# Loading the last job's feed-forward weights in units of 1024 columns

## The chip, the cores and the metric

The kernel runs on one core of one Trainium2 chip. The metric is device time in microseconds of one execution; each kernel is run several times and the median counts. The core has a matrix engine (TensorE, PE; its weight loads are listed apart as PEld), a vector engine (VectorE, DVE), a scalar engine (ScalarE, ACT), GpSimd (POOL) and a queue engine (SyncE, SP) that issues most of the DMA transfers. All transfers run on 16 DMA engines that the queues share.

## What is computed

Two layers, each an attention with a recurrent memory followed by a gated feed-forward block, with the same weights in both layers:

```python
def _A_ref(x, mem0, Wq, Wk, Wv, Wo, seg_len):      # S = 2048, D = 576, H = 32, Dh = 128, M = 8, seg = 32
    mem = mem0
    for s in range(n_seg):                          # 64 segments, one after another
        h = concat([mem, x[segment s]])             # 40 rows
        q, k, v = h @ Wq, h @ Wk, h @ Wv
        p = softmax(where(mask, q @ k.T * scale, -1e9))
        o = (p @ v) @ Wo
        mem = o[:, :M]                              # handed to the next segment
        outs.append(o[:, M:])
def _B_ref(x, w1, w3, w2):                          # F = 4608
    return (silu(x @ w1) * (x @ w3)) @ w2

x = x + _A_ref(_layernorm(x), ...); x = x + _B_ref(_layernorm(x), ...)
x = x + _A_ref(_layernorm(x), ...); x = x + _B_ref(_layernorm(x), ...)
```

All inputs are bfloat16; `w1` and `w3` are 576 x 4608 and `w2` is 4608 x 576.

## The kernel before

The attention is a chain over 64 segments, so the kernel runs it in steps: step t works on segment t of the first layer and, eight steps later, on segment t - 8 of the second. There are 72 steps, 0 to 71; the last eight have the second layer alone. `step` builds the nodes of one step: QK (queries and keys of 32 heads in four groups of 8 heads; each group's main matmuls read chunks 0 to 7 of the tile W, QKt its chunk 8), SC (scores), softmax on DVE and ACT, TR (transpose), PV, WO (the output projection, one node for each group, WO0 to WO3) and VM/VX (values, from the tile WV).

The feed-forward block works on 128 rows at a time, in jobs (`job`). F is cut into 18 pairs of 128-column blocks (`pr`, 0 to 17); a node FF makes gate and up for one pair (16 matmuls over four 128-row chunks, 32 when its columns are split), FFt adds the last 64 of the 576 rows (4 matmuls), ACT and DVE make the product in HTT, and W2b multiplies two pairs (one `pp`) by `w2`. For most jobs the weights of one pair are brought by `load_w13` (two transfers of 256 KB, two of 32 KB into the tile W13) and `load_w2` (288 KB into W2C), in two buffers each.

The last job cannot start before the last step's attention is done. By then Wq and Wk in the tile W and Wv in the tile WV are no longer read, and the kernel loads most of the last job's weights over them. `tail_load(i, what, gate)` does it in eight units i of 512 columns (two pairs): `what` 0 brings W1 and W3 into the columns `i * 512` on of W, chunks 0 to 3 and 4 to 7, with the 64-row remainders in the two halves of chunk 8; `what` 1 brings W2 into WV. Unit 0 serves pairs 0 and 1, unit 7 pairs 14 and 15. Pairs 16 and 17 stay in W13 and W2C from the job before. The job before also uses unit 0, for its own last two pairs.

What holds a tail transfer: the reads of the old contents (QK of the group of heads in those columns; a group has 1024 columns of W, two units), the lane of its completion semaphore (SP's transfers take eight in turn, so a ninth waits for the landing of the first), and for `what` 0 a gate. The gate is a manual dependence of the unit's first transfer on a matmul node of the last step: unit 0 has none, unit 1 waits for WO1, units 2 to 7 for WO3. The order on TensorE is written out by hand, as letters in `FIRST`, `FOUR` and `LAST`; the orders of the other engines and of SP come from `plan`, which places each node at its earliest time by the given costs and priorities. Line 659 is the helper of every matmul, 662 of ACT, 665 of DVE, 668 of the transfers on SP.

Of the kernel before, what the change touches and what calls it, by code (L numbers as in the profile page):

```python
# [13 lines left out]
P = 128  # L14
R64 = 64
D = 576
# [231 lines left out]
def make_nodes(em, nseg, pools, o=Opt, dma_bw=230e3, load_bw=345e3):  # L248
# [4 lines left out]
    def node(*a, **k):  # L253
        n = Node(*a, **k)
        n.prio += 1e-9 * len(nodes)
        nodes.append(n)
        return n
# [5 lines left out]
    kb = lambda rows, cols: rows * cols * 2  # L263
# [9 lines left out]
    def load(name, nbytes, prio, fn, deps=()):  # L273
        return node("DMA", nbytes / load_bw, fn, deps=deps, prio=prio, name=name, lat=2.0)
# [208 lines left out]
    tail = []  # L483
# [3 lines left out]
    def job(j):  # L487
# [6 lines left out]
        s0 = 4 * j + 4 if j < ngrp else 4 * j - 4 + LAG  # L494
# [74 lines left out]
        if last:  # L569
            v_done, qk_done = last_reads  # L570
            me = steps[nst - 1]
            gates = {1: me["WO1"], **{i: me[f"WO{NG - 1}"] for i in range(2, 8)}}
            for i in range(8):
                g = gates.get(i)
                tail.append([load("tail", kb(128, c), s0 + o.tail_at + 0.01 * i, em.tail_load(i, what, g), deps=dep + [g])
                             for what, c, dep in ((0, 9 * 512, qk_done[i]), (1, 4 * 576, v_done))])
            shared.pop()()
        norm()
        if last:
# [29 lines left out]
    for t in range(nst):  # L609
        if t % 4 == 2 and (t + 2) // 4 < ngrp:  # L610
            x_in((t + 2) // 4)
        if t == LAG:
            ht_mem[t].append(node("DVE", 0.1, em.init_mem(1, LAG), deps=[m0e] + reads_ht.get(LAG - R_HT, []), prio=LAG - 2, name="m0"))
        if role(t) == 0 or t == 0:
            vx_pair(t - role(t), t - 1 + o.vx)
        step(t)
        if t % 4 == 1 and t // 4 < ngrp:
            x_res(t // 4)
        if t % 4 == 3:
            job((t + 1) // 4 - 1)  # L620
        elif t == nst - 1:
            job(nst // 4)
# [12 lines left out]
class Emitter:  # L635
# [139 lines left out]
    def tail_load(self, i, what, gate):  # L775

        def f(n):
            T = self.T
            fa = i * 512
            t13, t2 = T.W[:, :, fa:fa + 512], T.WV[:, i * 4 * D:(i + 1) * 4 * D].rearrange("p (b d) -> p b d", b=4)  # L780
            held = gate and what == 0

            def dma(*x):
                nonlocal held
                self.dma(*x)
                if held:
                    held = False
                    self.tc.add_manual_dep(self.last["SP"].ins, gate.inst.ins.name, self.pace_dep, reason="pace of the loads")

            if what == 0:  # L790
                for kind, wd in ((0, self.a.w1), (1, self.a.w3)):
                    dma(t13[:, 4 * kind:4 * kind + 4], wd[0:4 * P, fa:fa + 512].rearrange("(c p) f -> p c f", p=P))
                for kind, wd in ((0, self.a.w1), (1, self.a.w3)):
                    dma(t13[kind * R64:(kind + 1) * R64, 8], wd[4 * P:D, fa:fa + 512])
            else:
                dma(t2, self.a.w2[fa:fa + 512, :].rearrange("(b p) d -> p b d", p=P))
            for h in range(2):
                self.tail_w[2 * i + h] = (t13[:, :, h * 2 * P:(h + 1) * 2 * P], t2[:, 2 * h:2 * h + 2])
        return f
# [637 lines left out]
```

## Time and profile before

| what | us |
|---|---|
| median of 3 runs (lowest, highest) | 2650.18 (2648.84, 2653.23) |
| profiled execution | 2657.81 |
| its span, first to last instruction | 2656.0 |
| TensorE busy in the span | 2578.3 |
| VectorE busy | 2004.1 |
| ScalarE busy | 1242.3 |

The mean granted clock of TensorE was 0.992 of full speed. Times in the views below are microseconds from the start of the span. In the chain of waits each row has its start, its length and what the end of the kernel waited for then; "issue" is time in which the engine waited for nothing that the profile shows. In the timeline a row gives start, length, engine, line, operation, tiles and number of instructions, and in brackets the idle time before it with what ended it. In the DMA rows q1 is the queue of data transfers from SP and ACT, q8 that of instruction blocks; numbers are packets, MB and the share of the 16 engines. In the rows of stretches the busy time of each engine follows the length, then the granted clock, the DMA share and GB/s.

### The profile page before, as it was taken

The page shows a single profiled execution, that of the slowest core. Times are in us where ns is not written, and L with a number is a line of the kernel's source. Part 1 is how long each engine was busy: PE and PEld are TensorE (multiplying, and loading weights), DVE is VectorE, ACT ScalarE, POOL GpSimd, SP SyncE. Part 2 cuts the span into 40 slices and gives each one's busy share as a digit, 9 for nine tenths or more (in the row PEclk, how much of TensorE's full clock was granted, in tenths as well). Part 3 has the DMA queues.
Part 4 walks back from the last instruction along what each step waited for, and adds up shares of the span by engine and source line. Part 5 has one row for each costly group of instructions (what it writes and reads, how often), then busy time and mean ns, then how long its engine had stood idle before and what let it go on. Part 6 is the DMA issues. An engine that isn't in the chain of part 4 may idle for free.

```text
span 2656.0 us, 133410 instructions
## 1 busy us (share of the span) xinstructions
PE 2578.3 (97%) x59426; PEld 2216.6 (83%) x59426; DVE 2004.1 (75%) x5137; ACT 1242.3 (47%) x3495; POOL 335.2 (13%) x399
## 2 busy tenths in 40 slices
PE   6899999999999999999999999999999999999998
PEld 4788878888888888888888888888888888888887
DVE  4677777877787778778777877877787787777866
ACT  2555453444545444454544544454444445454443
POOL 1111111110101111010101101110110111011110
PEclk8899999999999999999999999999999999999999
DMA  9055746556554655555465555645565554554458
GB/s 322 4 153 150 182 101 152 128 131 157 117 141 108 152 135 126 155 128 139 109 143 134 138 146 125 146 106 151 122 147 139 132 140 106 129 139 131 130 155 244
DMA packets 690433, 371.48 MB, mean 140 GB/s; under 512 B 234328, under 2 KB 682592, under 8 KB 689216
## 3 DMA queue, kind: packets, MB, share of 16 engines
q1 hardware_dynamic: 686320, 355.08, 53.5%
q8 instruction: 464, 7.60, 1.2%
q0 software_dynamic: 3024, 6.93, 0.9%
q10 hardware_dynamic: 512, 0.94, 0.2%
q14 instruction: 113, 0.93, 0.1%
HBM read 306.72 MB, written 2.36 MB: 116 GB/s over the span
## 4 chain that ended last, share of the span: by engine, by line
PE 83%; DMA 9%; DVE 5%; ACT 1%; issue 1%; SPq 1%; POOL 0%; ACTq 0%; DVEq 0%; POOLq 0%
PE bank L659 83%; DMA PTS<-PB 5%; DMA W<-in_B_w_dram 1%; DMA W2C<-in_B_w_dram 1%; DVE STAT L665 1%; DMA WV<-in_A_Wv_dram 1%; DVE SME L665 1%; DVE PB L665 1%; SPq L668 1%; DVE V L665 0%; DMA W<-in_A_Wq_dram 0%; ACT V L662 0%; DVE XR L665 0%; DVE HTT L665 0%; DVE LNS L665 0%
## 5 line engine op out<-in xcount | busy, mean ns | idle before, releaser
L659 PEld LDWEIGHTS <-W 128*128 128x128 bf16 (+2 forms) x32464 | 1259.9, 100 | 118.1 <-issue 63.6
L659 PE MATMUL bank<-HT,W 128*128 128x80 bf16 (+3 forms) x23040 | 785.1, 197 | 16.1 <-issue 9.3
L659 PE MATMUL bank<-XTB,W 128*64 128x256 bf16 (+5 forms) x9424 | 658.9, 263 | 2.0 <-DMA W<-in_B_w_dram 2.0
L1093 POOL MEMSET PB<- 128x1024 bf16 x288 | 273.9, 951 | 1944.4 <-DMA PTS<-PB 1142.8
L662 ACT ACTIVATE QKT<-bank 128x256 bf16<-128x256 f32 (+4 forms) x1423 | 342.4, 320 | 246.4 <-PE bank L659 216.9
L659 PE MATMUL bank<-OT,WO 128*128 128x80 bf16 (+3 forms) x11520 | 421.2, 199 | 1.0 <-ACT OT L662 0.5
L662 ACT ACTIVATE V<-bank 64x512 bf16<-64x512 f32 (+1 forms) x605 | 339.6, 585 | 164.9 <-PE bank L659 158.4
L659 PEld LDWEIGHTS <-WO 128*128 128x128 bf16 (+1 forms) x11520 | 387.8, 102 | 34.0 <-issue 18.7
L659 PE MATMUL bank<-WV,HT 128*32 128x512 bf16 (+4 forms) x3768 | 370.4, 386 | 5.1 <-DMA WV<-in_A_Wv_dram 4.5
L659 PE MATMUL bank<-W2C,HTT 128*64 128x288 bf16 (+1 forms) x3216 | 321.8, 287 | 3.4 <-DMA W2C<-in_B_w_dram 2.8
L662 ACT ACTIVATE OT<-bank 128x320 bf16<-128x320 f32 x374 | 153.8, 437 | 313.2 <-PE bank L659 309.3
L665 DVE TENSOR_REDUCE STAT<-SME 104x8 f32<-104x320 f32 (+1 forms) x576 | 275.1, 478 | 27.9 <-ACT SME L662 22.3
L665 DVE TENSOR_TENSOR PB<-SME,STAT 40x128 bf16<-40x128 f32 (+4 forms) x912 | 275.4, 336 | 12.1 <-DVE STAT L665 0.4
L665 DVE SCALAR_TENSOR_TENSOR HTT<-HTT,bank 128x512 bf16<-128x512 bf16 (+1 forms) x324 | 201.5, 622 | 106.7 <-ACT HTT L662 103.7
L659 PEld LDWEIGHTS <-HT 128*32 128x32 bf16 (+4 forms) x3768 | 155.4, 100 | 145.2 <-issue 39.1
L659 PEld LDWEIGHTS <-HTT 128*64 128x64 bf16 (+1 forms) x3288 | 230.1, 105 | 40.8 <-issue 7.3
L662 ACT ACTIVATE HTT<-bank 128x512 bf16<-128x512 f32 (+1 forms) x324 | 173.9, 548 | 179.9 <-PE bank L659 178.3
L665 DVE SCALAR_TENSOR_TENSOR XR<-bank,XR 128x288 f32<-128x288 f32 x574 | 241.5, 447 | 14.4 <-PE bank L659 11.0
L662 ACT ACTIVATE SME<-SME 104x320 f32<-104x320 f32 (+1 forms) x288 | 135.1, 469 | 241.4 <-DVE SME L665 238.1
L665 DVE TENSOR_TENSOR HTT<-HTT,bank 128x512 bf16<-128x512 bf16 (+1 forms) x324 | 203.7, 629 | 33.0 <-PE bank L659 0.5
L665 DVE CAST QKT<-bank 128x192 bf16<-128x192 f32 (+2 forms) x497 | 141.4, 328 | 104.7 <-PE bank L659 102.5
L665 DVE CAST V<-bank 64x512 bf16<-64x512 f32 (+1 forms) x259 | 177.3, 684 | 36.9 <-PE bank L659 33.0
(60 smaller groups left out, 1394.4 us busy)
## 6 DMA issues: line engine op xcount, KB each, us to landing
W<-in_B_w_dram SPq DMA_DIRECT2D x608, 256.0 KB, 3.9
W2C<-in_B_w_dram SPq DMA_DIRECT2D x304, 288.0 KB, 3.5
W<-in_B_w_dram SPq DMA_DIRECT2D x608, 32.0 KB, 3.9
W<-in_B_w_dram SPq DMA_DIRECT2D x16, 512.0 KB, 8.3
WO<-in_A_Wo_dram SPq DMA_DIRECT2D x4, 1152.0 KB, 10.0
XR<-in_A_x_dram POOLq DMA_DIRECT2D x16, 288.0 KB, 4.0
WV<-in_B_w_dram SPq DMA_DIRECT2D x8, 576.0 KB, 7.3
W<-in_A_Wq_dram SPq DMA_DIRECT2D x16, 256.0 KB, 5.8
```

The source lines that it names most:

```text
L659: self.ch("PE", self.nc.tensor.matmul(out, lhsT=lhsT, rhs=rhs, start=start, stop=stop, skip_group_check=True, **k))
L662: self.ch("ACT", self.nc.scalar.activation(*a, **k))
L665: self.ch("DVE", getattr(self.nc.vector, fn_)(*a, **k))
L668: self.ch("SP", self.nc.sync.dma_start(out=out, in_=in_))
L1093: return lambda n: self.ch("POOL", self.nc.gpsimd.memset(self.T.PB[:, pb.i, 0:GROUPS[g][1]], 0.0))
```

## The change

W1 and W3 of the last job are loaded for two units at once: 1024 columns, in four transfers of two 128-row blocks each (512 KB, rows of 2 KB) and two of 64 rows (128 KB), instead of twice two transfers of four blocks (512 KB, rows of 1 KB) and two of 64 rows (64 KB). The even unit's node does it with the even unit's gate; unit 1's gate on WO1 is gone. Both units of a pair depend on the wide load. W2 is loaded by unit as before.

```diff
@@ job
             for i in range(8):
                 g = gates.get(i)
-                tail.append([load("tail", kb(128, c), s0 + o.tail_at + 0.01 * i, em.tail_load(i, what, g), deps=dep + [g])
-                             for what, c, dep in ((0, 9 * 512, qk_done[i]), (1, 4 * 576, v_done))])
+                if i % 2 == 0:
+                    wide = load("tail", kb(128, 9 * 1024), s0 + o.tail_at + 0.01 * i, em.tail_load(i, 0, g), deps=qk_done[i] + qk_done[i + 1] + [d for d in [g] if d])
+                tail.append([wide, load("tail", kb(128, 4 * 576), s0 + o.tail_at + 0.01 * i, em.tail_load(i, 1, g), deps=v_done + [d for d in [g] if d])])
@@ tail_load
             if what == 0:
+                wide = T.W[:, :, fa:fa + 1024]
                 for kind, wd in ((0, self.a.w1), (1, self.a.w3)):
-                    dma(t13[:, 4 * kind:4 * kind + 4], wd[0:4 * P, fa:fa + 512].rearrange("(c p) f -> p c f", p=P))
+                    for c in (0, 2):
+                        dma(wide[:, 4 * kind + c:4 * kind + c + 2], wd[c * P:(c + 2) * P, fa:fa + 1024].rearrange("(c p) f -> p c f", p=P))
                 for kind, wd in ((0, self.a.w1), (1, self.a.w3)):
-                    dma(t13[kind * R64:(kind + 1) * R64, 8], wd[4 * P:D, fa:fa + 512])
+                    dma(wide[kind * R64:(kind + 1) * R64, 8], wd[4 * P:D, fa:fa + 1024])
```

The order in which the transfers are issued on SP changes with it. Before: W of unit 0, W13 of pair 17, WV of unit 0, W2C of pairs 16 and 17, W of unit 1, WV of unit 1, W of unit 2, WV of unit 2, and so on. After: W of units 0 and 1, W13 of pair 17, W2C of pairs 16 and 17, WV of units 0 and 1, W of units 2 and 3, WV of units 2 and 3, and so on.

## The prediction, made before the result was known

> **What bounds the kernel now.** I read the page first, then the last 70 us, because nothing before the last step's QK changes.
>
> ```profile
> span 2656.0 us, 133410 instructions
> PE 2578.3 (97%) x59426; PEld 2216.6 (83%) x59426; DVE 2004.1 (75%) x5137; ACT 1242.3 (47%) x3495; POOL 335.2 (13%) x399
> ...
> q8 instruction: 464, 7.60, 1.2%
> ...
> W<-in_B_w_dram SPq DMA_DIRECT2D x16, 512.0 KB, 8.3
> ...
> WV<-in_B_w_dram SPq DMA_DIRECT2D x8, 576.0 KB, 7.3
> ```
>
> TensorE is busy 97% of the span; a load matters only where TensorE waits for it. The x16 and x8 rows are the last job's W1/W3 and W2, all in the tail. The chain of waits from 2586 us on, in order of time, shows where TensorE stood still there:
>
> ```profile
> 2590.55 0.17 issue
> 2590.72 4.86 PE bank L659 x128
> 2595.59 1.07 issue
> 2596.66 3.37 PE bank L659 x128
> 2600.03 2.02 issue
> 2602.05 3.10 PE bank L659 x45
> ...
> 2640.24 7.90 DMA W<-in_B_w_dram
> 2648.13 0.05 issue
> 2648.18 1.39 PE bank L659 x20
> ```
>
> Two things are seen. At the end, a W transfer issued at 2640.24 lands 7.90 us later and TensorE resumes at 2648.18. Earlier, three "issue" stops (0.17, 1.07, 2.02) lie exactly 128 matmuls apart. 118,852 weight loads and matmuls (line PE) over the 464 packets of queue q8 are 256 instructions a packet, 128 matmuls with their weight loads: TensorE runs out of instructions and waits for the next block. When that block travelled is read from DMA views of narrow stretches, the first two of 2590.8:2594.1 and 2594.1:2595.5, the others of 2596.7:2599.7, 2599.7:2600.9 and 2602.1:2604.3 us:
>
> ```profile
> q1 hardware_dynamic: 1023, 1.02, 92.7%
> q1 hardware_dynamic: 672, 0.39, 106.0%
> q8 instruction: 1, 0.02, 5.0%
> q1 hardware_dynamic: 720, 0.67, 78.6%
> q8 instruction: 1, 0.02, 4.8%
> q8 instruction: 1, 0.02, 2.7%
> ```
>
> After 2590.72 no block moves for 3.4 us while q1 moves 1023 packets; it comes in the second stretch. After 2596.66 none moves for 3.0 us until q1 is nearly empty. After 2602.05, with q1 silent, the block is there within 2.2 us. I read this as: the data burst at 2588 to 2600 us holds up the instruction blocks, just where QK's short matmuls use 128 in 3.4 us. These stops are worth more than the one at the end.
>
> **The change, part by part.** SP's order before (its queue, tail):
>
> ```profile
> 2588.45 7.24 SPq L668 DMA_DIRECT2D W<-in_B_w_dram  x8
> 2595.79 0.53 SPq L668 DMA_DIRECT2D WV<-in_B_w_dram  x1
> 2604.43 0.89 SPq L668 DMA_DIRECT2D W2C<-in_B_w_dram  x2
> 2608.01 2.89 SPq L668 DMA_DIRECT2D W<-in_B_w_dram  x4
> 2610.95 0.59 SPq L668 DMA_DIRECT2D WV<-in_B_w_dram  x1
> 2612.87 2.12 SPq L668 DMA_DIRECT2D W<-in_B_w_dram  x4
> ```
>
> The order of instructions on PE, ACT, DVE and POOL is the same in both kernels; on SP eight transfers fewer are issued (10 to 8 for each pair of units) and the order is: wide 0/1 (4 x 512 KB + 2 x 128 KB), W13 of pair 17, W2C x2, WV 0 and 1, then wide 2/3 with WV 2 and 3, and so on. Eight issues at 0.9 us (7.24 us for x8) leave SP, which is not on the path: nothing.
>
> *The removed gate.* Unit 1's W (1.18 MB) no longer waits for WO1 at 2608.01; it leaves at about 2590, in the burst. Its two columns of units belong to one group of eight heads, so the first wide transfer waits for all 64 QK matmuls of that group instead of the first half: 0.8 us later (32 more at 26 ns, 3.37 us for 128), on SP only.
>
> *Rate.* The opening loads 2 KB rows of Wq and Wk; the tail loads 1 KB rows of W and 1152 B rows of WV:
>
> ```profile
> 14.00:22.00 8.00, 7.27 (x101) 4.02 (x101) 0.49 (x1) 1.73 (x6) 0.00 (x0) 1.00 1.05 373
> 2616.00:2646.00 30.00, 30.00 (x488) 25.17 (x483) 22.13 (x56) 7.96 (x20) 1.13 (x2) 1.00 1.09 336
> 2602.70:2606.10 3.40, 3.08 (x42) 2.24 (x39) 2.65 (x8) 2.02 (x6) 1.53 (x2) 0.50 0.17 29
> ```
>
> (last three columns: clock, DMA share, GB/s). So 336 GB/s is the lower bound for the wide units and 373 the upper; I take 373 for W, whose rows become those of the opening.
>
> *The end.* After WO3's gate at 2612.87 six units remain: 10.6 MB, of which the last two WV (1.18 MB) follow the last W. With 3 us until the first has landed, the last W lands at 2612.87 + 3 + 9.4/0.373 = 2641.1, or 2643.9 at 336. Before, it landed at 2648.13. TensorE needs it here:
>
> ```profile
> 2643.67 2.29 PE L659 MATMUL bank<-XTB,W 64*128 64x128 bf16 x40
> 2645.80 1.14 PE L659 MATMUL bank<-WV,HTT 128*128 128x288 bf16 x8
> 2646.87 0.29 PE L659 MATMUL bank<-XTB,W 64*128 64x128 bf16 x4
> 2648.18 2.50 PE L659 MATMUL bank<-XTB,W 64*128 64x128 bf16 x40 [1.02 <-DMA W<-in_B_w_dram]
> ```
>
> Units 6 and 7 now come together, so the need is the first of unit 6 at about 2643.8; even the slow bound costs only 0.1 us there. The wait of 1.02 us goes: bounds 0.9 and 1.02, taken 1.0. Nothing replaces it: from 2616 to 2646 TensorE is busy 30.00 of 30.00 us, so earlier data make nothing else earlier. Earlier units have more room: wide 4/5 (5.9 MB after the gate) lands by 2612.87 + 3 + 17.6 = 2633.5 at 336, needed at 2637.35 by the first matmuls of unit 4.
>
> *What is moved back.* W13 of pair 17 goes behind 1.18 MB more, 3.2 us. Its reader is in the group that starts at 2614.56; SP had issued it by 2595.7 (the x8 row); with the 8.3 us to landing of the far larger W it lands by 2604.0, and 3.2 us later by 2607.2. WV 0 goes behind the W2C pair, which waits for TensorE until 2604.43: issued at 2605.3 with WV 1, landed by about 2613 with 7.3 us from the page; its first reader starts at 2621.44. Both cost nothing, and would only if the loads were 8 us later still.
>
> ```profile
> 2614.56 3.31 PE L659 MATMUL bank<-XTB,W 64*128 64x128 bf16 x108
> 2620.14 1.15 PE L659 MATMUL bank<-W2C,HTT 128*64 128x288 bf16 x16
> 2621.44 1.15 PE L659 MATMUL bank<-WV,HTT 128*128 128x288 bf16 x8
> ```
>
> *The instruction blocks.* The burst now holds wide 0/1 and W13 (2.95 MB) instead of unit 0, W13 and WV 0 (2.36 MB). At 373 GB/s for W it is 0.59/0.373 - 1.18 x (1/0.336 - 1/0.373) = 1.6 - 0.35 = 1.2 us longer, but it waits less on issue, since SP issues 8 transfers over 7.24 us now. Bounds for the two stops together: both vanish (-3.1 us, as with q1 silent) or each grows by the whole extra W (2 x 3.2 us). I take 0: the block after 2590.72 has about the same bytes ahead of it, and the burst ends within about 1 us of where it did.
>
> *The clock.* Behind the 2.02 us stop the granted clock is 0.50 for 3.4 us with 3.08 us busy; at full clock that work is half, so the window costs 1.5 us. It stays if the stop stays: 0, bounds -1.5 and +1.5 (a second such window).
>
> **The sum.** The profiled execution took 2657.81 us, 1.8 us around its span of 2656.0. Less 1.0 it is 2656.8. The median of the three runs, 2650.18, lies 7.6 us below the profiled time; I carry the difference over: 2650.18 - 1.0 = 2649.2.
>
> **The rivals.**
> 1. *The burst hurts less.* Fewer and longer packets let the blocks through; these stops and the half-clock window go: 1.0 + 3.1 + 1.5 = 5.6, 2644.6; half of that gain on the stops gives 2647. For it: the block at 2602.1:2604.3 came quickly on a silent queue, and the wide W are through sooner per byte. Against: more bytes stand in the same place.
> 2. *The burst hurts more (slower).* The gate on unit 1 kept 1.18 MB out of QK's stretch. If the next blocks wait behind the bytes queued before them, each stop grows by the net extra (1.6 us, W's 3.2 less WV 0's 1.6), and a second window falls to half clock: -1.0 + 3.2 + 1.5 = +3.7, 2653.9; with the full 3.2 us each, +6.9, 2657.1. It decides for slower from 1.0 us of added stop on. For it: the second block came only when q1 had drained. Against: the first came in the middle of the stream.
> 3. *A block waits behind a number of packets, not of bytes.* Packets of 2 KB then double the 3.4 and 3.0 us: -1.0 + 6.4 + 1.5 = +6.9, 2657.1 here too. Against: the opening runs 2 KB rows with TensorE busy 7.27 of 8.00 us, though with longer matmuls.
> 4. *The change does nothing.* The end is held by something else, or the profiled run, 7.6 us longer than the median, made the 1.02 us and the plain runs have none: 2650.2. Against: the wait names W, and the transfer's landing at 2648.14 meets it to 0.04 us.
>
> The Trainium skill ("DMA: Bandwidth & Descriptors", Queues, rings and completion order) says that a DMA engine goes round-robin between its queue rows, changing at packet boundaries, a packet being typically 9 to 17 descriptors. By that rule a block waits for one packet of data: an estimate from that page is 17 x 1 KB at 336/16 GB/s, 0.8 us, and 1.6 us with 2 KB rows, so that two stops would add 1.6 us at most and the sum would be 2650.8. The waits of 3 us and more above are longer than the rule makes them: the trace does not bear it out as the whole cause.
>
> **How the numbers follow.** Chances: forecast 0.47, rival 1 0.20, rival 2 0.22, rival 3 0.05, rival 4 0.06. The forecast's own range is 2648 to 2651. The range runs to 2645.0 (rival 1 nearly whole) and 2654.5 (rival 2 with the net extra). I take 0.2%, 5.3 us, as what a measurement of this kernel can tell from no change. Faster than 2644.9 needs rival 1 whole: 0.13. Slower than 2655.5 needs rival 2 near its upper price or rival 3: 0.15. Within: 0.72.
>
> **What would show it.** Right: no wait of TensorE on W after 2640 us; the last W landing 4 to 7 us before its reader; the stops 128 matmuls apart at 2590 to 2602 us within 1 us of 0.17, 1.07 and 2.02 in sum; one half-clock window. Rival 1: these stops and that window gone. Rivals 2 and 3: stops of 3 us or more, a second half-clock window, or new "issue" stops at 2605 to 2625. Wrong altogether: TensorE waiting on W, W2C or WV between 2614 and 2645.

## The result, and the profile after

| kernel | median us (lowest to highest, runs) | profiled span |
|---|---|---|
| before | 2649.98 (2645.96 to 2655.14, 21) | 2656.0 |
| changed | 2653.79 (2648.17 to 2658.2, 21) | 2656.4 |

The ratio is 1.0016, 95% interval 1.001 to 1.0022: the change costs 3.8 us where 1.0 us of gain was forecast. From the page of the changed kernel, the span and the lines of the last job's W1/W3 and W2 (count, size, us to landing). Its helper lines are numbered one higher than before (660 for every matmul, 669 for the transfers on SP); in the kernels of the experiments they stand up to three higher.

```profile
span 2656.4 us, 133369 instructions
...
W<-in_B_w_dram SPq DMA_DIRECT2D x16, 512.0 KB, 8.9
...
WV<-in_B_w_dram SPq DMA_DIRECT2D x8, 576.0 KB, 8.9
```

The two spans differ by 0.4 us, not by 3.8. A profile is one run of many, and the 21 of each kernel spread over 9 to 10 us, so the spans alone say little: the profiled run of before, at 2657.81 us, is longer than any of those 21, and that of the changed kernel, at 2658.20, is the longest of its 21. Besides, in the changed kernel's profile the last step's QK began 1.6 us earlier (2585.61 against 2587.21 us). From that start to the end of the span it is 70.80 us, and 68.84 before. The chain of waits of the changed kernel in that stretch (start, length, what the end waited for):

```profile
2583.99 9.71 PE bank L660 x297
2593.70 1.35 issue
2595.05 3.37 PE bank L660 x128
2598.42 2.84 issue
2601.26 3.13 PE bank L660 x45
...
2610.12 1.89 PE bank L660 x69
2612.01 0.75 issue
2612.76 0.76 PE bank L660 x27
...
2614.30 35.65 PE bank L660 x567
```

The last row is what the change was expected to bring: TensorE runs from 2614.30 to 2649.95 without waiting for a load. The "issue" rows are what it cost. At QK they are 1.35 and 2.84 (4.19 in sum, 3.26 before), and a new one of 0.75 stands in the output projection of the last group, 69 matmuls into a row of 96. The queue of SP (start, length, transfers) and the DMA views of four stretches, 2589.2:2592.5, 2592.5:2593.7, 2607.6:2610.4 and 2610.4:2611.6 us, show what moved at the time. The first and third stretch have one DMA row each, the second and fourth two:

```profile
2587.94 7.29 SPq L669 DMA_DIRECT2D W<-in_B_w_dram  x10
2603.66 0.89 SPq L669 DMA_DIRECT2D W2C<-in_B_w_dram  x2
2604.60 1.01 SPq L669 DMA_DIRECT2D WV<-in_B_w_dram  x2
2613.02 3.90 SPq L669 DMA_DIRECT2D W<-in_B_w_dram  x6
```

```profile
q1 hardware_dynamic: 724, 1.21, 101.6%
q1 hardware_dynamic: 227, 0.44, 99.5%
q8 instruction: 1, 0.02, 5.7%
q1 hardware_dynamic: 715, 0.80, 92.9%
q1 hardware_dynamic: 145, 0.15, 36.7%
q8 instruction: 1, 0.02, 4.6%
```

For 3.3 us of the burst q1 moves 1.21 MB and no block comes; then one does. The same happens again at 2607.6: the W2C pair and both WV loads (1.77 MB, issued from 2603.66 to 2605.6) fill the DMA engines for 2.8 us, and the block that TensorE needs at 2612.01 starts only at 2610.44, when they are nearly through. Before, WV of unit 0 had gone earlier, and the block wanted there, at about 2607.7, started at 2608.16 on a silent queue. The stretches of the changed kernel (length, PE, PEld, DVE, ACT, POOL busy, granted clock, DMA share, GB/s) give the clock and the rate:

```profile
2601.90:2605.30 3.40, 3.08 (x42) 2.24 (x38) 2.63 (x8) 1.98 (x6) 1.50 (x2) 0.50 0.15 27
2615.50:2618.90 3.40, 3.40 (x73) 3.40 (x70) 2.92 (x9) 0.77 (x2) 0.55 (x1) 0.50 1.04 378
2616.00:2645.00 29.00, 29.00 (x454) 24.55 (x451) 20.16 (x51) 7.31 (x18) 1.13 (x2) 0.95 1.06 350
2636.00:2645.20 9.20, 9.20 (x141) 7.92 (x139) 6.83 (x18) 2.09 (x6) 0.00 (x0) 1.00 1.05 336
```

A second window of half clock lies behind the new stop, with TensorE busy all through it: 3.40 us for work of 1.7. The rate is 350 GB/s over the tail and 336 at its end, against 336 before, not 373. So the last W of units 6 and 7, their 64-row remainders, landed at 2645.2. The first reader is among unit 6's 64-row matmuls, in the row that starts at 2645.45:

```profile
2644.37 1.14 PE L660 MATMUL bank<-WV,HTT 128*128 128x288 bf16 x8
2645.45 2.29 PE L660 MATMUL bank<-XTB,W 64*128 64x128 bf16 x40
```

No wait stands before the second row, with 0.2 to 0.4 us to spare. TensorE came there 59.84 us after the start of QK, and 56.46 before (2643.67 less 2587.21). Of these 3.4 us 1.75 held back the gate of the loads as well (27.41 us from QK's start to SP's issue, 25.66 before); the other 1.6, the new half-clock window's, gave them the room.

### The profile page after: what moved, and what is told of

Same layout as the page of the kernel before. It is cut to its first block, busy times and chain, and to the rows that moved or that the text cites. A ratio compares the mean times of both kernels' runs of the same rounds, so it can differ in the third digit from the quotient of the medians.

```text
span 2656.4 us, 133369 instructions
## 1 busy us (share of the span) xinstructions
PE 2573.8 (97%) x59393; PEld 2215.2 (83%) x59426; DVE 2003.3 (75%) x5137; ACT 1242.8 (47%) x3495; POOL 335.2 (13%) x399
## 3 DMA queue, kind: packets, MB, share of 16 engines
HBM read 306.72 MB, written 2.36 MB: 116 GB/s over the span
## 4 chain that ended last, share of the span: by engine, by line
PE 86%; DMA 7%; DVE 4%; ACT 1%; issue 1%; POOL 0%; SPq 0%; ACTq 0%; DVEq 0%; POOLq 0%
PE bank L660 86%; DMA PTS<-PB 4%; DMA W2C<-in_B_w_dram 1%; DMA WV<-in_A_Wv_dram 1%; DVE STAT L666 1%; DMA W<-in_B_w_dram 1%; DVE SME L666 1%; DVE PB L666 1%; DMA W<-in_A_Wq_dram 0%; DVE V L666 0%; ACT V L663 0%; ACT PTS L663 0%; DVE QKT L666 0%; POOL PB L1096 0%; DVE LNS L666 0%
## 5 line engine op out<-in xcount | busy, mean ns | idle before, releaser
L666 DVE SCALAR_TENSOR_TENSOR XR<-bank,XR 128x288 f32<-128x288 f32 x574 | 241.3, 447 | 16.5 <-PE bank L660 13.1
```

Source lines behind the costliest of these rows:

```text
L666: self.ch("DVE", getattr(self.nc.vector, fn_)(*a, **k))
```

## The experiments

Eleven runs followed: both kernels once more, and nine others. Their tails stand side by side in microseconds, from one profile each: "issue" stops between the start of the last step's QK and the job before's last W2b, "issue" stops after that, waits of TensorE for W, half-clock time ahead of the last W2b group, and the length from QK's start to the end of the span. The ratio is to runs of the kernel before on the same chip; "one run" has none. The profiled run is seldom the median one: c2's took the longest time of its eleven, c3's the shortest, a2's the second shortest of twelve. So the columns show what stood still in one run, and the ratio is what the kernel costs.

| kernel | ratio (95% interval) | QK stops | later stops | waits for W | half clock | tail |
|---|---|---|---|---|---|---|
| before | 1 | 3.26 | 0 | 1.02 | 3.4 | 68.84 |
| c0, before again | one run | 0.80 | 1.18 | 0 | 0 | 65.69 |
| changed | 1.0016 (1.001 to 1.0022) | 4.19 | 0.75 | 0 | 6.8 | 70.80 |
| b1, changed again | 1.0023 (1.001 to 1.0035) | 4.36 | 0.69 | 1.17 | 3.4 | 70.90 |
| a1, gate only | 1.0004 (0.9992 to 1.0016) | 4.94 | 0 | 0 | 10.2 | 70.47 |
| a2, first pair as before | 1.0009 (0.9997 to 1.0021) | 1.52 | 0.66 | 0.72 | 0 | 66.87 |
| a3, W2 held | 1.0023 (1.0013 to 1.0033) | 4.01 | 0 | 5.86 | 10.2 | 76.27 |
| a4, rows of 1 KB | 1.0020 (1.0008 to 1.0032) | 2.60 | 0 | 2.82 | 6.8 | 71.18 |
| b2, first pair wide only | 1.0018 (1.0006 to 1.003) | 4.35 | 1.30 | 0 | 6.8 | 71.62 |
| b3, burst later | 0.9998 (0.9986 to 1.0009) | 0 | 1.41 | 0 | 0 | 65.29 |
| b4, wide burst later | 1.0012 (1.0003 to 1.0022) | 0.44 | 1.70 | 1.14 | 3.4 | 68.85 |
| c2, W2 as before | 1.0015 (1.0006 to 1.0024) | 5.22 | 0 | 3.16 | 13.6 | 75.12 |
| c3, W2 moved only | 1.0000 (0.9989 to 1.0012) | 0.96 | 1.57 | 0 | 3.4 | 67.20 |

**Both kernels again (c0, b1).** No edit.

> The kernel before once more, for a second profile. Theory A (data in flight hold up the instruction blocks): stops at QK of 1.5 to 3.5 us in sum, no issue stop at the last group's output projection, since no W2 load runs beside its block. Theory C (the stops vary from run to run and the profiles shown so far differ by chance): stops as in the changed kernel, 4 us or more, and one of 0.7 us or more at that projection.

> The changed kernel once more, for a second profile of it and a second interval. Theory A (data in flight in QK's stretch and again after it hold up TensorE's instruction blocks): the issue stops at QK again sum to 3.5 to 5 us against 3.3 in the kernel before, one more stands where the moved W2C and W2 loads run, and the ratio is 1.001 to 1.0025. Theory B (the pair's first reader needs all 1024 columns, so the end wait is not removed but stands on a margin of nothing): TensorE waits for W at unit 6's first matmul, 0 to 3 us, in a profile where the loads are slower; the ratio is the same. Rival (the first profiles differ by chance, neither is the cause): stops at QK of 3.3 us or less, no end wait, and a ratio of 0.9995 to 1.0005.

c0 took 2651.31 us. Its chain has two stops (beside one of 0.10), and its "waits by engine" one row for both (total, times, longest):

```profile
2591.94 0.80 issue
...
2610.56 1.18 issue
```

```profile
PE bank L659 <- issue: 2.0, 2, 1.2
```

QK's stops are 0.80 here, below the 1.5 to 3.5 of theory A and far below the 4 of theory C, and a stop stands later, in the 108 matmuls on XTB. So the first profile of the kernel before, on which the prediction rests, is at QK the worse of the two. The changed kernel repeats itself: 4.36 at QK, 0.69 at the projection. But the wait for W is back, in its timeline at another place, unit 6's first matmuls (brackets: idle time, what ended it):

```profile
2644.41 0.23 PE L660 MATMUL bank<-XTB,W 64*128 64x128 bf16 x1 [0.96 <-DMA W<-in_B_w_dram]
2644.85 2.17 PE L660 MATMUL bank<-XTB,W 64*128 64x128 bf16 x35 [0.21 <-DMA W<-in_B_w_dram]
```

With two profiles of each, the tail is 67.3 us before (68.84 and 65.69) and 70.9 after: 3.6 us, and the medians differ by 3.8. By stage, means of two: QK 14.3 to 16.5 (+2.2), from there to the last step's end 9.9 to 11.3 (+1.4), all the rest +0.0 within 0.1. The loss lies at QK and behind it up to the projection: of the 1.4 there 0.7 is the new stop, and most of the other half is the half-clock window behind QK, which both profiles of the changed kernel have and one of the kernel before. The end gives nothing back on balance. The 2.2 at QK rests on the second profiles as well: between the first two the stops grew by 0.9 alone.

**The gate alone (a1).**

```diff
-            gates = {1: me["WO1"], **{i: me[f"WO{NG - 1}"] for i in range(2, 8)}}
+            gates = {i: me[f"WO{NG - 1}"] for i in range(2, 8)}
```

> The kernel before with unit 1's gate on WO1 taken away and nothing else; loads stay in units of 512 columns with 1 KB rows. Unit 1's W (1.18 MB) then stands in the burst behind unit 0, W13 and WV 0, so that the burst is 3.5 MB. Theory A (data in flight holds up the instruction blocks): the two stops during QK (before 1.07 and 2.02 us, after the change 1.35 and 2.84) become at least as long as after the change, the second up to 5 us, and the time is 2652 to 2657. Theory B (rows of 2 KB are what harms): stops as before, time 2648 to 2651. Theory C (the later place of WV 0 and 1 alone): as before too.

In units of 512 columns, W of unit 1 in the burst brought stops of 2.72 and 2.22 at QK and 10.2 us at half clock; the end wait went. The chain:

```profile
2596.84 2.72 issue
2599.57 4.00 PE bank L659 x128
2603.56 2.22 issue
```

The stops are theory A's; its time, 2 to 7 us more, is not: the ratio is 1.0004, and neither 1 nor the changed kernel's 1.0016 is excluded. The tail of this profile is 3.2 us longer than the mean of the two before; that the plain runs lose less is not explained.

**Where the wide load costs: at the first pair (b2) or at the others (a2).** a2 loads units 0 and 1 as before, with the gate, and units 2 to 7 wide; b2 the other way round.

In `tail_load` the transfers follow the same condition. The nodes of a2, against the changed kernel:

```diff
-                if i % 2 == 0:
+                if i < 2:
+                    wide = load("tail", kb(128, 9 * 512), s0 + o.tail_at + 0.01 * i, em.tail_load(i, 0, g), deps=qk_done[i] + [d for d in [g] if d])
+                elif i % 2 == 0:
```

and of b2:

```diff
-                if i % 2 == 0:
+                if i > 1:
+                    wide = load("tail", kb(128, 9 * 512), s0 + o.tail_at + 0.01 * i, em.tail_load(i, 0, g), deps=qk_done[i] + [d for d in [g] if d])
+                elif i == 0:
```

> The changed kernel, but units 0 and 1 are loaded as before (512 columns, unit 1 gated on WO1, W2 of unit 0 ahead of W2C); the other six units stay wide. Theory A: stops during QK as before (3.1 us together), no stop of 0.75 us at WO3, one half-clock window, and the 1.0 us wait for W at the end gone: 2648 to 2649.5, a little below before. Theory B (2 KB rows): new stops on instruction blocks between 2614 and 2640 us, time at or above 2652.

> The wide load for units 0 and 1 only (no gate, so the same burst and the same moved loads as in the changed kernel); units 2 to 7 in 512 columns as before. Theory A alone: the early loss stays (ratio 1.0005 to 1.0015 from QK and the second half-clock window, and the end wait for W of about 1 us is back, so 1.0015 to 1.002 in all). Theory B alone: the loss is at the end of the wide units, so this one is at 1.000 (0.9995 to 1.0005), and its last W is waited for by about 1 us as in the kernel before.

b2 has the whole early loss (4.35 at QK, 1.30 at the projection, two half-clock windows) and the changed kernel's ratio, 1.0018, although its end is clean. a2 has stops like those of the kernel before (1.52), and its own wait for W at unit 6's first matmuls, so the gain that theory A expected of it did not come. Its ratio of 1.0009 does not exclude 1. By the medians the early part carries most of the loss, though the two intervals overlap; b2 and a2 (4.5 and 1.8 us by their medians) add up to 6.3, near the 6.1 by which b1 was behind (3.8 in the first measurement).

**Rows of 1 KB (a4).** The changed kernel's order and bytes, W in transfers of four blocks of 512 columns.

```diff
-                    for c in (0, 2):
-                        dma(wide[:, 4 * kind + c:4 * kind + c + 2], wd[c * P:(c + 2) * P, fa:fa + 1024].rearrange("(c p) f -> p c f", p=P))
+                    for h in (0, 512):
+                        dma(wide[:, 4 * kind:4 * kind + 4, h:h + 512], wd[0:4 * P, fa + h:fa + h + 512].rearrange("(c p) f -> p c f", p=P))
```

> The changed kernel with the same transfers in the same order and of the same size, but each of the four 512 KB ones is 512 columns of four row blocks (1 KB rows) in place of 1024 columns of two. Theory A (bytes in flight): same as the changed kernel or up to 1 us longer, since the burst moves more slowly: 2653 to 2655. Theory B (a block waits behind a number of packets, so that 2 KB rows double its wait): the stops during QK fall below those of before, time 2649 to 2651.

Ratio 1.0020, near the changed kernel's: shorter rows take nothing of the loss away. Its QK stops are smaller (2.60, with one of 0.98 just ahead of QK that the column leaves out), but its W for units 6 and 7 came 2.82 us after need (the x36 row is unit 6's first):

```profile
2653.54 3.88 PE L660 MATMUL bank<-XTB,W 64*128 64x128 bf16 x36 [2.82 <-DMA W<-in_B_w_dram]
```

**The moved W2 loads (a3, c2, c3).** a3 and c2 are the changed kernel with W2 of units 0 and 1 behind WO3 (a3), or about where it was before (c2: unit 0's straight behind the wide load, unit 1's behind WO1); c3 is the kernel before with nothing but these two loads moved to their new place.

a3, against the changed kernel (the gate is then put on WV of unit 0, the first of the two):

```diff
-                tail.append([wide, load("tail", kb(128, 4 * 576), s0 + o.tail_at + 0.01 * i, em.tail_load(i, 1, g), deps=v_done + [d for d in [g] if d])])
+                tail.append([wide, load("tail", kb(128, 4 * 576), s0 + o.tail_at + 0.01 * i, em.tail_load(i, 1, gates[2] if i < 2 else g), deps=v_done + [gates[2] if i < 2 else g])])
```

c2, against the changed kernel (WV of unit 1 carries the gate):

```diff
-                tail.append([wide, load("tail", kb(128, 4 * 576), s0 + o.tail_at + 0.01 * i, em.tail_load(i, 1, g), deps=v_done + [d for d in [g] if d])])
+                w2g = me["WO1"] if i == 1 else g
+                tail.append([wide, load("tail", kb(128, 4 * 576), s0 + o.tail_at + 0.01 * i - 9 * (i == 0), em.tail_load(i, 1, w2g), deps=v_done + [d for d in [w2g] if d])])
```

c3, against the kernel before:

```diff
-                tail.append([load("tail", kb(128, c), s0 + o.tail_at + 0.01 * i, em.tail_load(i, what, g), deps=dep + [g])
-                             for what, c, dep in ((0, 9 * 512, qk_done[i]), (1, 4 * 576, v_done))])
+                late = [] if i > 1 else [n for n in nodes if n.name == "W2l"][-2:]
+                tail.append([load("tail", kb(128, 9 * 512), s0 + o.tail_at + 0.01 * i, em.tail_load(i, 0, g), deps=qk_done[i] + [g] + late * (i == 1)),
+                             load("tail", kb(128, 4 * 576), s0 + o.tail_at + 0.01 * i - (i == 1), em.tail_load(i, 1, g), deps=v_done + late + [g] * (i > 1))])
```

> The changed kernel with W2 of units 0 and 1 held until WO3 as the next wide load is (it goes ahead of it), so that only the W2C pair moves between 2603 and 2613 us. Theory A: the stop of 0.75 us at 2612 us goes, and with it probably the half-clock window at 2615.5 (1.6 us); the stops during QK stay at 1.35 and 2.84: 2650.5 to 2652.5, some 1.5 to 2.5 us below the changed kernel. If the burst at QK is all of the loss: no change, 2653 to 2654.5.

> The changed kernel with W2 of units 0 and 1 loaded where the kernel before does it: unit 0's straight behind the wide load, unit 1's behind the gate on WO1. The burst at QK grows from 2.95 to 3.54 MB. Theory A1 (the early loss comes from the moved W2 loads, by the stop at the last output projection and the second half-clock window): that stop of 0.7 us and the window behind it go, ratio 0.9998 to 1.0006 less whatever the end wait takes (0 to 1.2 us). Theory A2 (it comes from the larger burst at QK): the QK stops stay at 4.2 us or grow to 5, ratio 1.0012 to 1.0025.

> The kernel before with nothing but W2 of units 0 and 1 moved to where the changed kernel has them, behind the W2C pair; all W in 512 columns and the gate as before. The burst at QK shrinks from 2.36 to 1.77 MB. Theory A1: a stop of about 0.7 us at the last output projection and a second half-clock window of 3.4 us (1.6 us lost), ratio 1.0004 to 1.0012. Theory A2: QK stops fall from 3.3 to 1 to 2 us, ratio 0.999 to 1.0002.

With the loads away from 2604 to 2610, in a3 and c2, the stop at the projection is gone; in c3 it is there, 1.57, though all W is in 512 columns with the gate (W of unit 1 runs right behind the two loads there, 1.18 MB more in that stretch). Chains of c3 and of c2:

```profile
2587.12 0.80 issue
...
2601.09 1.57 issue
```

```profile
2595.11 1.35 issue
2596.46 3.88 PE bank L661 x128
2600.34 3.70 issue
```

So the new stop comes with the loads in that stretch. It isn't the whole loss: c3's burst is 0.59 MB smaller, its QK stops are 0.96, and its ratio is 1.0000. c2 has 3.54 MB in the burst, QK stops of 5.22 and 10.2 us of half clock there, no stop at the projection, and 1.0015. Of the theories A1 and A2 these runs favour A2, that the loss comes with the larger burst at QK. They don't settle it: c3's interval reaches 1.0012, c2 lost 3.16 us to W at its end besides, and a1, with as large a burst as c2, stands at 1.0004. In a3 the last W had the 1.18 MB of the two loads more ahead of it and was 5.08 us late; c2's was late by 3.16:

```profile
2651.84 4.20 PE L660 MATMUL bank<-XTB,W 64*128 64x128 bf16 x36 [5.08 <-DMA W<-in_B_w_dram]
```

```profile
2649.33 3.85 PE L661 MATMUL bank<-XTB,W 64*128 64x128 bf16 x36 [3.16 <-DMA W<-in_B_w_dram]
```

**The burst behind QK (b3, b4).** One gate more in the kernel before (b3) and in the changed one (b4):

```diff
-            gates = {1: me["WO1"], **{i: me[f"WO{NG - 1}"] for i in range(2, 8)}}
+            gates = {0: me[f"QK{NG - 1}"][-1], 1: me["WO1"], **{i: me[f"WO{NG - 1}"] for i in range(2, 8)}}
```

> The kernel before with one gate more: unit 0's W is issued behind the last QK matmuls, so nothing but W13 of pair 17 moves while QK runs; everything of 512 columns as before. Theory A: the issue stops at QK fall from 3.3 us to under 1 us, the half-clock window behind them goes (1.5 us), and the ratio is 0.998 to 0.999 (3 to 5 us less). Theory B says nothing of QK: ratio 0.9995 to 1.0005. Rival to A (the stops come from QK's own rate of instructions, 128 matmuls in 3.4 us, and not from the data): the stops stay at about 3 us, ratio 1.000.

> The changed kernel with the first wide load (units 0 and 1, 2.36 MB) issued behind the last QK matmuls. Theory A alone: the QK stops and their window go as in the run with 512 columns, the end wait is gone too, ratio 0.9978 to 0.999, below the same gate with 512 columns. Theory B: the wide units still stand on no margin at the end, a wait for W of 1 to 5 us at the first reader of units 4 or 6 takes part of it back: ratio above that of the same gate with 512 columns, 0.999 to 1.0015.

With only W13 of pair 17 moving under QK, its stops are gone in b3 and 0.44 in b4, and QK's stage takes 12.0 and 12.6 us (15.6 and 13.1 in the two profiles of the kernel before). The stops are the data's doing, not QK's pace alone. But the loads now run under the next short matmuls, those on XTB, and a stop stands there, as in c0 and a2; b3's chain:

```profile
2605.43 3.26 PE bank L659 x100
2608.69 1.41 issue
2610.09 31.07 PE bank L659 x467
```

Its ratio is 0.9998, not the 0.998 to 0.999 that theory A expected: its tail of 65.29 is 2.0 below the mean of the two before, and only 0.4 below c0's. A gain of 2 us is within the interval, and so is none. b4 is 1.0012: the pair's first reader waited 0.99 + 0.15 for W, and the projection 1.70 for its block. No version was shown to beat the kernel before.

## Why the prediction was wrong

*The instruction blocks, taken as 0.* This is the step that failed, and it decided the sign: the second block was judged by the first, and the term measured is +2.2 us. "The block after 2590.72 has about the same bytes ahead of it, and the burst ends within about 1 us of where it did" looked at the first block alone. Its stop did stay (1.35 in the changed kernel, 1.07 in b1, 1.07 before). The burst's end moved by about 1 us, as said: read in slices of half a microsecond, its share of the DMA engines falls below a half 12.0 and 12.5 us after QK's start before, 13.0 and 13.5 after. But the second stop grew, 2.02 to 2.84 and again 2.84, and in c0 it had been next to nothing. The old burst thinned out just where TensorE asks for that block, 9 to 10.5 us after QK's start, and the larger one does not (before, c0, changed, b1; the last two columns are DMA share and GB/s):

```profile
2596.20:2597.70 1.50, 1.04 (x41) 1.04 (x42) 1.43 (x5) 1.49 (x3) 0.00 (x0) 1.00 0.72 148
2592.85:2594.35 1.50, 1.50 (x64) 1.50 (x64) 1.43 (x6) 1.46 (x4) 0.00 (x0) 1.00 0.87 150
2594.60:2596.10 1.50, 1.05 (x42) 1.05 (x43) 1.43 (x6) 1.46 (x4) 0.00 (x0) 1.00 1.06 357
2593.80:2595.30 1.50, 0.77 (x31) 0.77 (x32) 1.40 (x5) 1.45 (x4) 0.00 (x0) 1.00 1.06 382
```

In c0 the block started in this thin stretch, 1.15 us after TensorE had passed into the block ahead of it; in the first profile of before it did not and waited 3.15; in both of the changed kernel the burst, with W13 now at its end, filled the engines for 3.1 us more, and the block waited 3.6. Over two profiles each, QK's stops are 2.0 before and 4.3 after, +2.2 us, inside the prediction's bounds of -3.1 and +6.4, far from the value taken. Six further profiles order themselves by the bytes in the burst: 1.77 MB 0.96 (c3), 2.36 MB 1.52 (a2), 2.95 MB 4.35 and 4.01 (b2, a3), 3.54 MB 5.22 and 4.94 (c2, a1). a4, with 2.95 MB and 2.60, is the one that falls short. Chance may have helped this order, since the profiled times of c3 and a2 lie below their kernels' medians, and those of b2, a3, c2 and a1 above; b1's, with stops of 4.36, lies below.

*What is moved back, "both cost nothing".* No reader of W13, W2C or WV waited for them, as said. But the rule that the prediction had drawn from QK, that data on their way hold up a block, was not put to them at their new place, where they cost 0.75 and 0.69 us of stop. In c3 the same move in the old kernel brought a stop of 1.57, and no change of the time.

*The clock, taken as 0.* The changed kernel had two windows in its first profile and one in b1, the kernel before one and none: about one more, 1.5 to 1.7 us, the prediction's upper bound.

*The end, taken as -1.0.* The wait of 1.02 us at unit 7 went; it was not there to be won in every run, since c0 has none. A wait of 0 and 1.17 us at unit 6 stands in its place, since the first reader of the two units is 3.2 us earlier than unit 7's and needs the 64-row remainders, which come last. The prediction saw that need, but put the last W at 2641.1 by 373 GB/s; it landed at 2645.2, at 350 and, in the last stretch, 336 GB/s. Its slow bound of 2643.9 was too early as well. The formula had not been tried on the kernel before: 2612.87 + 3 + 10.0/0.336 gives 2645.7 for a W that landed at 2648.1. With those 2.4 us added the slow bound is 2646.3, 2.5 us behind the need at 2643.8, and the end would have stood as a possible loss. The sign of being right, the last W 4 to 7 us before its reader, was counted from unit 7's reader; from unit 6's, at 2643.8, the prediction's own landing times leave 2.7 us at most.

*The rivals.* Rival 2 is the one that came true, with its figure: 2653.9 forecast, 2653.79 measured. That agreement is luck, since its terms were off against each other. It had 3.2 us at QK (2.2 measured) and 1.5 for a second window (about right), and kept the gain of 1.0 at the end, which is not there on average; the moved loads' 0.7 it did not have, nor the 1.18 that the kernel before can lose in the matmuls on XTB. Rival 1 falls: the stops grew in sum. Rival 3 falls twice: the blocks waited 3.6 us each under the changed kernel's burst with its rows of 2 KB, 3.48 and 3.15 under that of 1 KB, where rival 3 doubles the wait, and a4 with 1 KB lost as much. Rival 4 falls by the ratio, but its reason holds in half: c0 had no wait for W.

The rule of the Trainium skill that the prediction weighed ("DMA: Bandwidth & Descriptors", Queues, rings and completion order: the queues take turns at packet boundaries) would have these waits at 1.6 us at most by the prediction's estimate. The runs have 2.5 to 5.0 us under a full burst at QK and do not bear it out.

What stays open is why TensorE's waits for the wide pairs differ so much (0, 0.72, 1.14, 1.17, 2.82, 3.16 and 5.86 us in the seven profiles with units 6 and 7 loaded together, at most 1.02 in the other six). a3 has a reason, its 1.18 MB more behind the gate. In a4 and c2 the last W landed 34.2 and 34.4 us after the gate, against 32.2 in the changed kernel and 32.4 in b1, at 327 and 331 GB/s over the tail against 350 and 344; for a4 its rows of 1 KB fit that, for c2 no run tells the chip, the order and chance apart. Open, too, is how the 3.8 us divide between QK and the projection: the stops are shown to come from the data in flight, by b3, b4 and the order above, but the ratios of a1 and b3 don't follow their stops closely enough to give each its share.

## What to carry to other kernels

Before a landing time is forecast for a changed load, work the same formula on the kernel before and see that it gives the landing that its trace shows. A load moved into another stretch is to be weighed against everything on the DMA engines there, instruction blocks included: bytes under a stretch of 26 ns matmuls cost TensorE time here even though nobody waited for the data. And two units merged into one load are needed when the first of them is.

## What was not expected of the hardware

With the burst filling the DMA engines at QK, the packet of a block started 2.5 to 5.0 us after TensorE had passed into the block ahead of it, on the steady stream behind 2615 us mostly 1.5 to 4.6, and with q1 silent up to 1.2; rows of 1 KB and of 2 KB made no difference that these profiles show. From the start of that packet to TensorE's next matmul it was 2.2 to 2.7 us (2594.20 to 2596.66 and 2599.81 to 2602.05 before, 2598.61 to 2601.26 and 2610.44 to 2612.76 after). A block whose 128 matmuls take less than the two together stopped TensorE for the rest: in the changed kernel 3.56 + 2.65 - 3.37 gives the 2.84 of QK's second stop. That met the blocks of QK, at 3.4 us, nearly always under a burst; those of the feed-forward behind 2620 us, at over 8, in none of these profiles.

In the first two profiles half-clock windows of 3.4 us stood behind 2.02 us of stop before and 2.84 after, but in the changed kernel one also came behind 0.75 and 0.76 close together, and none behind 0.69 and 0.76 in b1 or behind 1.18 in c0. What releases them is not settled here.
